# Halves of x, thirds of a transform, and an earlier v: one re-ordering of an attention and long-convolution kernel

## The chip, the cores and the metric

The kernel runs on one core of one Trainium2 chip. (Each run is marked fast or slow; slow means here that it took over 1.5% longer than the fastest run of the same kernel.) Times are device microseconds (us) of that core for one execution of the program.

Engine names: PE is TensorE (matmuls; PEld is its weight load), DVE is VectorE, ACT is ScalarE, POOL is GpSimd, SP is SyncE, whose queue (SPq) issues most DMAs. PSUM is the accumulator memory that PE writes; an "eviction" copies a PSUM tile out to SBUF.

## The reference, cut to what matters

Two independent layers share the launch. Part A is local attention (32 heads of 18 columns, 8 keys per query at distances 0, 2, ..., 14). Part B is a gated long convolution. The outputs are concatenated.

```python
# part A: x (2048 x 576), wqkv (576 x 1728)
q, k, v = split(x @ wqkv)
logits = einsum(q, k gathered at pos - 2*w) * scale        # w = 0..7
o = einsum(softmax(logits), v gathered at pos - 2*w) @ wo
# part B: q, k, v (2048 x 576), ssm_k (576 x 2048)
k_shift = sum over 4 taps of k shifted by t, times shift_k[:, t]
kv = k_shift * v
y = irfft(rfft(kv, 2*S) * rfft(ssm_k, 2*S))[:S] + kv * ssm_D  # computed in float32
return concat([o, q * y])
```

The kernel computes the Fourier transforms as matmuls with tables, in two stages with a trip through Dram between them. The names used below are these. The *first transform* is stage one, over the convolution kernel (k chunks, written to `Dk`) and over `kv` (x chunks, written to `Dx`), eight chunks each. A *k-transform step* (`kh_step`) is stage two of the convolution kernel. A *g step* is stage two of `kv`, the product with the kernel's transform, and the first stage back (tile `Y`, written to `Dy`). There are eight of each. A *P step* (`pv_step`) handles two position groups of the attention's weighted sum: VectorE forms two `P` products and PE sums and projects them.

## The kernel before

The front transposes all of x on PE, then runs 18 q/k matmul steps with the first transform's chunks mixed in. Cuts are marked `# ...`.

```python
for qtr in range(4):                     # all of x is transposed first
    for kp in range(3):
        # ... PE transposes into psA, ScalarE (kp == 1) or VectorE copies to xT

def s1_chunk(src, c2, Dd, vst_pool, add_d):          # one chunk of the first transform
    vst = vst_pool.tile([128, 2, 2 * D], BF16, name="vst")   # pool of 2 buffers
    for ch in range(3):
        ps = psb()                                   # 2 PSUM buffers
        # ... two matmuls
        nc.scalar.activation(vst[:, :, 384 * ch:384 * ch + 384], ps[:, :, 0:384], ACT.Copy)
    for dh, (d0, d1) in enumerate(DCH):
        nc.sync.dma_start(by_f1(Dd, dh, 4 * c2, 4), vst[...][:, :, d0:d1])

wraw = k2[1][...]     # landing place of v's weights: inside a tile of k
sraw = q2[1][...]     # landing place of the shift taps: inside a tile of q

def permute_wv():                                    # v's weights, columns re-ordered
    for kb in range(5):
        nc.scalar.activation(wv[...], wraw[...], ACT.Copy)

sk_step()             # load the taps to sraw, VectorE copies them to skb
load_wv()
permute_wv()
# ...
b_steps = [x chunk 0, k chunk 0, x chunk 1, k chunk 1, ...]
run(qk_steps, b_steps)                               # interleaves the two lists
```

The back half runs the logits with k-transform steps and twelve v steps mixed in, then the softmax, then the P and g steps:

```python
run([logit steps, 8], [ia_tables] + [all 8 kh_steps and v_steps 0..11])
softmax_a(0); softmax_a(1)
g_step(0)
for t2 in range(12, 16): v_step(t2)
halo()                                   # about 2 MB of v copied to neighbours' partitions
softmax_b(0); softmax_b(1)
run([at_step 0..3], [g_step(1)])         # at: the softmax result, transposed
# ...
run([pv_step 0..2], [g_step 2..5])
run([pv_step 3..4], [g_step 6..7])
run([pv_step 5..7], [y_step 0..7])
```

## Time and profile before

The time was 295.15 us (median of 3 runs, 294.57 to 296.24). I cut the span at three events which any version of the kernel has: the first logit product on VectorE, the start of the softmax (the addition of the mask), and the first `P` product.

| phase | ends at (us) | length (us) |
|---|---|---|
| front: loads, q/k, first transform | 107.8 | 107.8 |
| logits | 156.6 | 48.8 |
| softmax, up to the first P product | 190.3 | 33.7 |
| tail | 294.6 | 104.3 |

The page of before opens with the span and each engine's busy time; its second part shows the same busy time in tenths for 40 slices of 7.4 us, with PEclk, the granted TensorE clock, below.

```profile
span 294.6 us, 5101 instructions
...
PE 241.2 (82%) x2129; PEld 152.6 (52%) x2129; DVE 201.3 (68%) x188; ACT 167.5 (57%) x242; POOL 25.9 (9%) x60
...
PE   1579269999997779999999455379999999997993
...
PEclk9999859999999778999999857558999999998999
```

PE is the busiest engine, so the reader should look for where it is *not* busy: at the start, at slices 4 and 5 (counted from 0), around slices 12 to 14, and in the softmax (slices 22 to 25).

The windows view of before gives busy time by phase (start:end, length, then busy time and instruction count of PE, PEld, DVE, ACT and POOL, the granted clock, the DMA share and GB/s).

```profile
0.00:107.80 107.80, 83.49 (x457) 43.62 (x457) 61.65 (x75) 63.95 (x76) 8.75 (x32) 0.92 0.65 207
107.80:156.60 48.80, 47.26 (x486) 27.22 (x488) 43.22 (x31) 32.43 (x55) 0.00 (x0) 0.97 0.51 156
156.60:190.30 33.70, 19.09 (x152) 12.70 (x149) 25.19 (x33) 23.59 (x36) 13.44 (x23) 0.71 0.68 196
190.30:294.60 104.30, 91.37 (x1038) 69.06 (x1037) 71.26 (x53) 47.50 (x76) 3.74 (x5) 0.93 0.48 151
```

The logits phase keeps PE and VectorE both close to full (47.3 and 43.2 of 48.8 us).

The list of waits of before names the stall at slices 4 and 5 (engine, tile and line, whom it waited for, total us, times, longest).

```profile
PE psA L248 <- ACT q L251: 8.1, 1, 8.1
```

The timeline of before shows the cause (start, us, engine, line, operation, tile and source; in brackets the idle time before and what ended it).

```profile
32.29 5.95 ACT L309 ACTIVATE wv<-k 128x576 bf16<-128x576 bf16 x5 [4.15 <-DMA k<-in_A_wqkv_dram]
...
39.34 1.01 PE L248 MATMUL psA<-xT,wq 128*128 128x512 bf16 x2 [8.07 <-ACT q L251]
```

ScalarE first waited 4.15 us for v's weights, then permuted them for 5.95 us. Each engine has its "own instruction stream" (the Trainium skill, "Trainium Architecture — The Big Picture", "Inside one NeuronCore"), and here the trace shows what follows from the order within one: the q/k evictions behind the permutes came late, both PSUM buffers were full, and PE stood until 39.34 us with four q/k steps done.

The chain of waits of before (start, us, what) has one long transfer in the softmax, a `Dy` write that stood behind the halo copies.

```profile
169.52 11.23 DMA Dy<-Y
```

### The profile page before, as it was taken

Reading aid. Unit: us, or ns where it says so; the run is one execution under the profiler, and the core shown is the slowest. Engines: PE = TensorE matmul, PEld = TensorE weight load, DVE = VectorE, ACT = ScalarE, POOL = GpSimd, SP = SyncE. Lnnn points to the kernel's source line nnn. Section 1 sums busy time; section 2 is a strip of 40 time slices with the busy share of each in tenths; the row PEclk is TensorE's granted clock in tenths of the full one; section 3 lists DMA queues with packets and bytes.
Section 4 is the critical chain, followed back from the end, with each engine's and each line's share of the span. In section 5 each row is a group of like instructions: output and inputs, shape, how many; then the busy total and the mean of one; then the engine's idle time right before and its main releaser. Section 6 shows DMA issues by size and latency. Waiting matters only on the chain.

```text
span 294.6 us, 5101 instructions
## 1 busy us (share of the span) xinstructions
PE 241.2 (82%) x2129; PEld 152.6 (52%) x2129; DVE 201.3 (68%) x188; ACT 167.5 (57%) x242; POOL 25.9 (9%) x60
## 2 busy tenths in 40 slices
PE   1579269999997779999999455379999999997993
PEld 1464024555543336565547233168676766766782
DVE  3750895898771149899977991685879669694531
ACT  2422656668868662877877957323576585550311
POOL 8200000000000000000000845000000000012200
PEclk9999859999999778999999857558999999998999
DMA  7999623595555556653344198820442432559982
GB/s 232 360 323 305 234 77 144 178 285 163 160 162 160 160 160 184 222 148 94 103 148 145 40 278 221 283 82 0 123 146 110 149 127 94 184 154 309 328 255 80
DMA packets 42594, 52.37 MB, mean 178 GB/s; under 512 B 2174, under 2 KB 36686, under 8 KB 42445
## 3 DMA queue, kind: packets, MB, share of 16 engines
q1 hardware_dynamic: 39644, 47.04, 50.4%
q0 software_dynamic: 1264, 3.17, 4.3%
q10 hardware_dynamic: 1664, 1.84, 1.9%
q8 instruction: 16, 0.26, 0.3%
q14 instruction: 6, 0.05, 0.0%
HBM read 31.11 MB, written 18.87 MB: 170 GB/s over the span
## 4 chain that ended last, share of the span: by engine, by line
PE 50%; ACT 17%; DMA 16%; DVE 11%; issue 5%; SPq 1%; DVEq 0%; ACTq 0%
PE psA L248 9%; PE psA L235 7%; PE psB L279 6%; PE psA L556 5%; PE psB L454 5%; PE psA L569 5%; DMA out_dram<-m 4%; DMA xnat<-in_A_x_dram 4%; ACT Xc L457 4%; DMA Dy<-Y 4%; DMA k<-in_A_wqkv_dram 4%; PE psB L293 3%; PE psA L398 3%; ACT Y L503 3%; ACT vst L283 3%
## 5 line engine op out<-in xcount | busy, mean ns | idle before, releaser
L248 PE MATMUL psA<-xT,wq 128*128 128x512 bf16 x160 | 42.7, 407 | 8.7 <-ACT q L251 8.1
L556 PE MATMUL psA<-ident,P 128*128 128x128 bf16 (+1 forms) x640 | 46.2, 231 | 1.5 <-DVE P L547 1.4
L556 PEld LDWEIGHTS <-P 128*128 128x128 bf16 (+1 forms) x640 | 40.9, 107 | 8.4 <-issue 4.6
L547 DVE TENSOR_TENSOR P<-vX,at 128x4608 bf16<-128x4608 bf16 x16 | 40.1, 2550 | 4.3 <-PE psA L556 4.3
L283 ACT ACTIVATE vst<-psB 128x768 bf16<-128x768 f32 x48 | 36.3, 814 | 9.1 <-PE psB L279 8.0
L395 DVE TENSOR_TENSOR prod<-q,k 128x4096 bf16<-128x4096 bf16 x16 | 36.1, 2284 | 0.8 <-PE psA L398 0.6
L248 PEld LDWEIGHTS <-wq 128*128 128x128 bf16 x160 | 16.2, 103 | 27.8 <-issue 14.1
L454 PE MATMUL psB<-Wt,W 128*64 128x288 bf16 x256 | 28.0, 312 | 1.5 <-ACT Y L503 0.6
L560 ACT ACTIVATE xT<-psA 128x1024 bf16<-128x1024 f32 x8 | 8.2, 1024 | 34.8 <-PE psA L556 34.8
L500 PE MATMUL psB<-m,IAt 64*128 64x288 bf16 x128 | 14.9, 320 | 14.2 <-DVE m L493 7.6
L235 PE MATMUL psA<-wv,xT 128*128 128x288 bf16 x160 | 25.3, 294 | 0.3 <-ACT vX L237 0.3
L491 DVE TENSOR_TENSOR m<-Xc,Khat 128x2304 bf16<-128x2304 bf16 x8 | 10.8, 1356 | 18.6 <-ACT Xc L457 18.6
L503 ACT ACTIVATE Y<-psB 128x576 bf16<-128x576 f32 x32 | 18.9, 650 | 7.4 <-PE psB L500 6.1
L296 DVE COPY kTt<-psB 128x1152 bf16<-128x1152 bf16 x8 | 6.1, 758 | 24.0 <-PE psB L293 23.9
L569 PE MATMUL psA<-wv,xT 128*128 128x288 bf16 x160 | 22.3, 287 | 0.0
L235 PEld LDWEIGHTS <-xT 128*128 128x128 bf16 x160 | 18.8, 147 | 6.8 <-issue 6.8
L539 POOL DMA_DIRECT2D wv<-in_A_wo_dram x18 | 8.9, 501 | 151.7 <-PE psA L235 146.2
L457 ACT ACTIVATE Khat<-psB 128x576 bf16<-128x576 f32 x32 | 19.5, 653 | 3.4 <-PE psB L454 3.1
L587 DVE TENSOR_TENSOR m<-psB,Lsb 128x576 bf16<-128x576 f32 x16 | 11.4, 752 | 14.6 <-DMA out_dram<-m 8.2
L457 ACT ACTIVATE Xc<-psB 128x576 bf16<-128x576 f32 x32 | 19.6, 651 | 1.3 <-PE psB L454 1.1
L454 PEld LDWEIGHTS <-W 128*64 128x64 bf16 x256 | 12.7, 112 | 13.5 <-issue 11.9
L146 PE MATMUL psA<-ident,xnat 128*128 128x128 bf16 x80 | 9.5, 310 | 11.1 <-DMA xnat<-in_A_x_dram 10.0
(116 smaller groups left out, 331.2 us busy)
## 6 DMA issues: line engine op xcount, KB each, us to landing
Dx<-vst SPq DMA_DIRECT2D x16, 288.0 KB, 3.0
Dk<-vst SPq DMA_DIRECT2D x16, 288.0 KB, 3.0
Wt<-Dk SPq DMA_DIRECT2D x8, 576.0 KB, 3.8
Wt<-Dx SPq DMA_DIRECT2D x8, 576.0 KB, 3.9
Dy<-Y SPq DMA_DIRECT2D x8, 576.0 KB, 3.0
Wt<-Dy SPq DMA_DIRECT2D x8, 576.0 KB, 6.0
kX<-in_B_k_dram SPq DMA_DIRECT2D x3, 1008.0 KB, 5.2
vt<-in_B_v_dram SPq DMA_DIRECT2D x4, 576.0 KB, 8.3
```

Of the source, the lines that this page charges most:

```text
L235: nc.tensor.matmul(ps[:, di, 0:288], xTt[:, kb, t2, :], wv[:, kb, d0:d1], start=(kb == 0), stop=(kb == 4))
L248: nc.tensor.matmul(ps[:, u, :], wcols(kb, comp, ct), xT[:, kb, 512 * j:512 * j + 512], start=(kb == 0), stop=(kb == 4))
L279: nc.tensor.matmul(ps[:, ri, 0:384], T1[:, ri, :], sf[:, 384 * ch:384 * ch + 384], start=True, stop=not extra)
L283: nc.scalar.activation(vst[:, :, 384 * ch:384 * ch + 384], ps[:, :, 0:384], ACT.Copy)
L395: nc.vector.tensor_tensor(prod[:], q2[ct // 2][:], k2[ct // 2][:, :, sh:sh + S], ALU.mult)
L454: nc.tensor.matmul(ps[64 * hp:64 * hp + 64, im, 0:HD], W2[:, im, 8 * g + 2 * prl + hp].rearrange("p l f -> p (l f)"), Wt[:, 2 * prl + hp, ...
L457: nc.scalar.activation(dst[:, :, prl, :], ps[:, :, 0:HD], ACT.Copy, scale=scale)
L500: nc.tensor.matmul(ps[:, hp, 0:HD], IAt[64 * hp:64 * hp + 64, zi, 4 * g + prl, :], m1[64 * hp:64 * hp + 64, zi, prl, :], start=(zi == 0), ...
L503: nc.scalar.activation(Y[:, 2 * prl:2 * prl + 2, :], ps[:, :, 0:HD], ACT.Copy)
L547: nc.vector.tensor_tensor(P[:].rearrange("p w (d h) -> p w d h", h=H), vs, at[:, :, t2, :].unsqueeze(2).to_broadcast([128, W, DH, H]), ALU ...
L556: nc.tensor.matmul(oacc[0:csz, ci, 128 * u:128 * u + 128], Ps[u][:, wi, 128 * ct:128 * ct + csz], ident[:], start=(ci % 2 == 0 and u == 0 ...
L569: nc.tensor.matmul(pso[:, di, 0:288], oT[:, ct, t2, :], wot[:, ct, d0:d1], start=(ct == 0), stop=(ct == 4))
```

## The change

The intent: start q/k on half of x and so fill the 0 to 39 us stretch; weave the first transform in thirds so that its evictions are shared between ScalarE and VectorE, and PE and ScalarE no longer wait for each other in turn at the end of the front; put the wv permutes on GpSimd; let v and its halo copies lead the logits phase so that no halo copy stands in the softmax. Five of the eight k-transform steps are written after the logits to make room; in the compiled order four of them run in the softmax (16 of the 32 `Khat` evictions in the trace of after). The diffs here and below are shortened: helper lambdas and some lines are left out, and `...` marks a cut.

```diff
-    for qtr in range(4):
+    def x_tr(qtr):
 ...
+    x_tr(0)
+    x_tr(1)
 ...
+    def s1_part(src, key, c2, ch, Dd, add_d):       # one third of a chunk
+        if ch == 0:
+            vsts[key] = kvp.tile([128, 2, 2 * D], BF16, name="vst")
 ...
+        if ch == 1:
+            nc.vector.tensor_copy(vst[:, :, 384 * ch:384 * ch + 384], ps[:, :, 0:384])
+        else:
             nc.scalar.activation(vst[:, :, 384 * ch:384 * ch + 384], ps[:, :, 0:384], ACT.Copy)
 ...
-            nc.scalar.activation(wv[...], wraw[...], ACT.Copy)
+            nc.gpsimd.tensor_copy(wv[...], wraw[...])
 ...
     sk_step()
+    qk_steps[0]()
+    qk_steps[1]()
+    x_tr(2)
+    x_tr(3)
     load_wv()
     permute_wv()
 ...
-    run(qk_steps, b_steps)
+    # k and x thirds alternate: k0.0 x2.0 k0.1 x2.1 k0.2 x2.2 k1.0 ...; k transposed 2 chunks ahead
+    run(qk_steps[2:], parts)
 ...
-    run([logit steps], [ia_tables] + mixed)
+    vh = []
+    for c in range(4):
+        vh += v_steps[4 * c:4 * c + 4] + [lambda c=c: halo(c)]
+    run([logit steps], [ia_tables] + vh + [lambda i=i: kh_step(i) for i in range(3)])
 ...
     softmax_a(0)
     softmax_a(1)
+    kh_step(3)
     g_step(0)
-    for t2 in range(12, 16):
-        v_step(t2)
-    halo()
+    kh_step(4)
     softmax_b(0)
     softmax_b(1)
+    for i in range(5, 8):
+        kh_step(i)
     run([at_step 0..3], [lambda: g_step(1)])
```

The q/k tiles also move up in the allocation.

More of the change, by code (lines that the diff above doesn't have):

```diff
@@ L107 @@
     wq = wqp.tile([128, 5, 2 * D], BF16, name="wq")
+    qk = pool("qk", 1, "left")
+    q2 = [qk.tile([128, 2, S], BF16, name=f"q2_{i}") for i in range(2)]
+    k2 = [qk.tile([128, 2, PADL + S], BF16, name=f"k2_{i}") for i in range(2)]
+    qh = qk.tile([128, S // 2], BF16, name="qh")
+    kh = qk.tile([128, PADL + S // 2], BF16, name="kh")
     xin = pool("xin", 4, "left")
@@ L215 @@
     nc.vector.tensor_copy(maskb[:], mask_f[:])
-    tw.release()
-    xin.release()
-    qk = pool("qk", 1, "left")
-    q2 = [qk.tile([128, 2, S], BF16, name=f"q2_{i}") for i in range(2)]
-    k2 = [qk.tile([128, 2, PADL + S], BF16, name=f"k2_{i}") for i in range(2)]
-    qh = qk.tile([128, S // 2], BF16, name="qh")
-    kh = qk.tile([128, PADL + S // 2], BF16, name="kh")
     for i in range(2):
@@ L269, in qk_half_step @@
             nc.scalar.activation(kh[64:128, 0:PADL], ps[64:128, 0, 0:PADL], ACT.Copy)
-    def s1_chunk(src, c2, Dd, vst_pool, add_d):
+    vsts = {}
+    def s1_part(src, key, c2, ch, Dd, add_d):
         sf = src.rearrange("p t d -> p (t d)")
-        vst = vst_pool.tile([128, 2, 2 * D], BF16, name="vst")
-        for ch in range(3):
-            ps = psb()
-            for ri in range(2):
-                extra = add_d and c2 == 0 and ri == 0 and ch < 2
-                nc.tensor.matmul(ps[:, ri, 0:384], T1[:, ri, :], sf[:, 384 * ch:384 * ch + 384], start=True, stop=not extra)
-                if extra:
-                    n = 384 if ch == 0 else 192
-                    nc.tensor.matmul(ps[:, ri, 0:n], row0[:], Db[:, 384 * ch:384 * ch + n], start=False, stop=True)
-            nc.scalar.activation(vst[:, :, 384 * ch:384 * ch + 384], ps[:, :, 0:384], ACT.Copy)
-        for dh, (d0, d1) in enumerate(DCH):
-            nc.sync.dma_start(by_f1(Dd, dh, 4 * c2, 4), vst[:].rearrange("p r (t d) -> p (r t) d", t=2)[:, :, d0:d1])
@@ L287, in k_step @@
-    def k_step(c2):
-        kt = kpre.tile([128, 2, D], BF16, name="kTt", bufs=2)
-        ptr = pb.tile([128, 2, 1024], BF16, name="psB")
-        for u in range(2):
-            for db in range(5):
-                n = 128 if db < 4 else 64
-                nc.tensor.transpose(ptr[:, u, 128 * db:128 * db + n],
-                                    knats[db][0:n, :].rearrange("p (a b) -> p b a", b=NT)[:, 2 * c2 + u, :],
-                                    ident[0:n, 0:n])
-        nc.vector.tensor_copy(kt[:], ptr[:, :, 0:D])
-        s1_chunk(kt, c2, Dk, kvp, True)
+        if ch == 0:
+            vsts[key] = kvp.tile([128, 2, 2 * D], BF16, name="vst")
@@ new lines, in s1_part @@
+        vst = vsts[key]
+        ps = psb()
+        for ri in range(2):
+            extra = add_d and c2 == 0 and ri == 0 and ch < 2
+            nc.tensor.matmul(ps[:, ri, 0:384], T1[:, ri, :], sf[:, 384 * ch:384 * ch + 384], start=True, stop=not extra)
+            if extra:
+                n = 384 if ch == 0 else 192
+                nc.tensor.matmul(ps[:, ri, 0:n], row0[:], Db[:, 384 * ch:384 * ch + n], start=False, stop=True)
+        if ch == 1:
+            nc.vector.tensor_copy(vst[:, :, 384 * ch:384 * ch + 384], ps[:, :, 0:384])
+        else:
+            nc.scalar.activation(vst[:, :, 384 * ch:384 * ch + 384], ps[:, :, 0:384], ACT.Copy)
@@ L299 @@
+        if ch == 2:
+            for dh, (d0, d1) in enumerate(DCH):
+                nc.sync.dma_start(by_f1(Dd, dh, 4 * c2, 4), vst[:].rearrange("p r (t d) -> p (r t) d", t=2)[:, :, d0:d1])
     wraw = k2[1][:].rearrange("p a t -> p (a t)")[:, 0:5 * D].rearrange("p (k c) -> p k c", k=5)
@@ L308, in permute_wv @@
             p0 = 64 if kb == 4 else 0
-            nc.scalar.activation(wv[p0:128, kb, :].rearrange("p (d h) -> p d h", h=H),
-                                 wraw[p0:128, kb, :].rearrange("p (h d) -> p d h", d=DH), ACT.Copy)
+            nc.gpsimd.tensor_copy(wv[p0:128, kb, :].rearrange("p (d h) -> p d h", h=H),
+                                  wraw[p0:128, kb, :].rearrange("p (h d) -> p d h", d=DH))
     v_steps = [lambda t2=t2: v_step(t2) for t2 in range(NT)]
@@ L351, with x_part @@
     kvt = {}
-    def x_step(c2):
-        if c2 % 2 == 0:
+    def x_part(c2, ch):
+        if c2 % 2 == 0 and ch == 0:
             kvt[0] = kv_step(c2 // 2)
-        s1_chunk(kvt[0][:, 2 * (c2 % 2):2 * (c2 % 2) + 2, :], c2, Dx, kvp, False)
+        s1_part(kvt[0][:, 2 * (c2 % 2):2 * (c2 % 2) + 2, :], "x", c2, ch, Dx, False)
     sk_step()
+    qk_steps[0]()
+    qk_steps[1]()
+    x_tr(2)
+    x_tr(3)
     load_wv()
     permute_wv()
+    tw.release()
+    xin.release()
     kpre = pool("kpre", 1, "left")
@@ L368, with k_tr, k_part @@
     nc.gpsimd.dma_start(Db[:], B_ssm_D.partition_broadcast(128))
-    b_steps = [lambda c2=c2: x_step(c2) for c2 in range(8)]
-    for c2 in range(8):
-        b_steps.insert(2 * c2 + 1, lambda c2=c2: k_step(c2))
-    run(qk_steps, b_steps)
+    ktt = {}
+    def k_tr(c2):
+        ktt[c2] = kpre.tile([128, 2, D], BF16, name="kTt", bufs=3)
+        ptr = pb.tile([128, 2, 1024], BF16, name="psB")
+        for u in range(2):
+            for db in range(5):
+                n = 128 if db < 4 else 64
+                nc.tensor.transpose(ptr[:, u, 128 * db:128 * db + n],
+                                    knats[db][0:n, :].rearrange("p (a b) -> p b a", b=NT)[:, 2 * c2 + u, :],
+                                    ident[0:n, 0:n])
+        nc.vector.tensor_copy(ktt[c2][:], ptr[:, :, 0:D])
+    def k_part(c2, ch):
+        if ch == 0 and c2 == 0:
+            k_tr(0)
+            k_tr(1)
+        if ch == 0 and c2 + 2 < 8:
+            k_tr(c2 + 2)
+        s1_part(ktt[c2], "k", c2, ch, Dk, True)
+    parts = []
+    for c2 in range(2):
+        parts += [lambda c2=c2, ch=ch: x_part(c2, ch) for ch in range(3)]
+    for c2 in range(8):
+        for ch in range(3):
+            parts.append(lambda c2=c2, ch=ch: k_part(c2, ch))
+            if c2 < 6:
+                parts.append(lambda c2=c2, ch=ch: x_part(c2 + 2, ch))
+    run(qk_steps[2:], parts)
     kpre.release()
@@ L504, in g_step, with halo @@
         nc.sync.dma_start(by_rt(Dy, dh, g), Y[:])
-    mixed = []
-    for g in range(8):
-        mixed += [lambda g=g: kh_step(g)] + (v_steps[2 * g:2 * g + 2] if g < 4 else v_steps[g + 4:g + 5])
-    def halo():
-        nc.sync.dma_start(vX[1:113, 0:14, :], vX[0:112, 16:30, :])
-        nc.sync.dma_start(vX[113:128, 0:14, :], vX[112:127, 16:30, :])
-        nc.sync.dma_start(vX[0:1, 0:14, :], vX[0:1, 16:30, :])
-    run([lambda wi=wi: logit_step(wi) for wi in range(W)], [ia_tables] + mixed)
+    def halo(c):
+        lo = max(2, 4 * c)
+        src, dst = slice(14 + lo, 18 + 4 * c), slice(lo - 2, 4 * c + 2)
+        nc.sync.dma_start(vX[1:113, dst, :], vX[0:112, src, :])
+        nc.sync.dma_start(vX[112:128, dst, :], vX[111:127, src, :])
+        if c == 3:
+            nc.sync.dma_start(vX[0:1, 0:14, :], vX[0:1, 16:30, :])
+    vh = []
+    for c in range(4):
+        vh += v_steps[4 * c:4 * c + 4] + [lambda c=c: halo(c)]
+    run([lambda wi=wi: logit_step(wi) for wi in range(W)], [ia_tables] + vh + [lambda i=i: kh_step(i) for i in range(3)])
     lg.release()
```

## The prediction

> What bounds the kernel now. TensorE (PE) is busy 82% of the 294.6 us span (busy table), so I ask where it is not. The timeline shows four places. (1) 0 to 21 us: loads and transposes of x. (2) 31.3 to 39.3: q/k matmuls wait 8.1 us for a PSUM buffer (list of waits): ScalarE stood behind five wv permutes (5.95 us) whose load landed at 32.3. (3) 94 to 110: q/k work is used up, the first transform runs alone, PE and ScalarE alternate (0.81 us eviction, two PSUM buffers), VectorE is nearly idle. (4) 160 to 190: softmax, and Y evictions held 11.2 us by a Dy write behind 2 MB of halo copies (chain of waits). Elsewhere PE is full (50 to 90), or VectorE (41 us of logit products); after 205 PE repeats a period of 11.3 us, its own work.
>
> What the change does.
> - wv permutes go to GpSimd: stall (2) goes. But the compiled order also moves the copy of the shift taps to VectorE's tenth place, ahead of every x copy. Its load stands behind x and weights (4.4 MB at 320 GB/s: lands at 15 to 16 us), so x copies start near 17 instead of 7.4. I count: first two q/k steps 22 to 26; second half of x, mixed with tap products of 1.36 us, done by 32 to 33. PE then has two steps done where the old kernel had four, which stopped till 39. Net at 40 us: 2 to 3 us, not 8. GpSimd copies read SBUF while VectorE runs two-input products; the Trainium skill (SBUF — State Buffer, Who interferes with whom) says these block each other (no trace here shows it yet). It may delay the first kv tile by 2 to 4 us.
> - Thirds woven, the middle one evicted by VectorE (estimate 0.85 us), k transposed two steps ahead: PE work left at 33 us is 14 steps of 2.13, halves 5.5, 48 thirds of 0.33, eight k transposes of 1.17: 61 us, at the 95% seen in 50 to 83, 64; plus 5 for start and tail. First transform ends near 103, not 110: minus 6.
> - Logits: v leads, four k-transform steps instead of eight; VectorE needs 44 us. 46 to 47 instead of 48.8: minus 2.
> - Softmax: halo and v steps leave, four k-transform steps move in (16 evictions of 0.6). From last logit to first P product 33.8 us becomes 26.5 (ScalarE-bound): minus 7.
> - Given back: two g steps (3.9 us of PE each) done before the first P now fall in the PE-bound tail of 104 us: plus 3 to 6.
>
> Sum: about minus 11. Predicted 284 us, range 276 to 292. Chances: faster by over 2% 0.76, within 2% 0.21, slower 0.03.
>
> What would show each step: no 8 us q/k wait on ScalarE, but a VectorE wait of about 8 us for the taps, ending at 15 to 16; first q/k matmul at 21 to 23; x transposes finished at 31 to 34; first logit product at 99 to 104; softmax start to first P 25 to 28 us; no Dy write above 6 us; first P to the end 107 to 110.
>
> What would make it wrong: taps landing earlier (gain nearer 18); GpSimd copies far longer than 1 us each, delaying kv tiles and a k eviction near 42; staging buffers with 3 us writes stalling the thirds; more cold clock (0.5 to 0.8 after idle stretches); the tail absorbing the g steps, or y writes lengthening it.

## More of the kernel before

Last, VectorE's timeline of before around the first P product. The letter pattern of the tail is easiest to see here: the g products (`m`, four instructions for one g step) and the `P` products share VectorE in one fixed order.

```profile
186.34 1.36 DVE L491 TENSOR_TENSOR m<-Xc,Khat 128x2304 bf16<-128x2304 bf16 x1 [8.12 <-ACT Xc L457]
...
190.35 7.49 DVE L547 TENSOR_TENSOR P<-vX,at 128x4608 bf16<-128x4608 bf16 x3
202.12 5.03 DVE L547 TENSOR_TENSOR P<-vX,at 128x4608 bf16<-128x4608 bf16 x2 [4.29 <-PE psA L556]
208.51 1.36 DVE L491 TENSOR_TENSOR m<-Xc,Khat 128x2304 bf16<-128x2304 bf16 x1 [1.36 <-ACT Xc L457]
```

The whole order, with g written where the last of a g step's four products stands and P for one P product, is `ggg PPPPP g PP g PP g PP g PP g PPP`. Three g steps are multiplied before the first P.

## The result, and the profile after

The changed kernel took 311.03 us (median of 4 runs, 309.28 to 312.02); the kernel before, run beside it on the same chip, took 294.86 (292.07 to 296.24). The ratio is 1.0555, 95% interval 1.0464 to 1.0646: **slower by 5.5%**. A ratio here and below is the mean time of one kernel's fast runs over that of the other's fast runs of the same rounds, so it is not quite the ratio of the medians quoted.

| phase | before | after | forecast change | measured change |
|---|---|---|---|---|
| front | 107.8 | 117.1 | −6 | +9.3 |
| logits | 48.8 | 46.2 | −2 | −2.6 |
| softmax to first P | 33.7 | 27.2 | −7 | −6.5 |
| tail | 104.3 | 118.9 | +3 to +6 | +14.6 |

Two of four terms came out as forecast, one of them in part by luck (see front_only and back_only). The front has the wrong sign, and the tail is more than twice its upper bound.

The page of after:

```profile
span 309.4 us, 5117 instructions
...
PE 242.5 (78%) x2129; PEld 150.9 (49%) x2129; DVE 217.9 (70%) x204; ACT 153.6 (50%) x221; POOL 34.3 (11%) x65
...
PE   1039699999976659999981685598999999998664
...
PEclk9999799999999655999996578579999999999979
```

PE did the same work (242 against 241 us) in a longer span. The clock row now reads 6, 5 and 5 in slices 13 to 15, where before was at 7 or 8. The windows of after, by the same four phases:

```profile
0.00:117.10 117.10, 84.37 (x473) 44.30 (x474) 79.01 (x91) 50.27 (x59) 17.15 (x37) 0.93 0.61 192
117.10:163.30 46.20, 43.81 (x448) 28.30 (x448) 42.98 (x30) 24.22 (x41) 7.07 (x12) 0.93 0.50 147
163.30:190.50 27.20, 15.55 (x128) 8.40 (x128) 17.20 (x25) 23.21 (x36) 6.38 (x12) 0.69 0.60 183
190.50:309.40 118.90, 98.74 (x1080) 69.90 (x1079) 78.72 (x60) 55.88 (x89) 3.75 (x5) 0.92 0.48 152
```

In the tail PE has 7.4 us more work (98.7 against 91.4), about the two g steps that the prediction named. But the phase is 14.6 us longer.

The list of waits of after has three entries that matter in the front. The old 8.1 us wait of the q/k matmuls is gone from it.

```profile
PE psA L152 <- DVE xT L157: 14.0, 5, 10.5
...
DVE skb L322 <- DMA q<-in_B_shift_k_dram: 11.3, 1, 11.3
...
ACT vst L291 <- DMA Dk<-vst: 8.6, 4, 2.3
```

The first two are one event: VectorE waited 11.3 us for the taps, in front of the copies of x, and PE waited 10.5 us for those copies. (In before VectorE waited 9.4 us for the taps too, but behind all copies of x.) The prediction had this one. The third, an eviction into a staging buffer that waits for that buffer's last write to reach Dram, it had only as a risk. The chain of waits of after runs through it:

```profile
81.57 5.37 DMA Dk<-vst
87.04 0.82 ACT vst L291
...
101.05 3.00 DMA Dk<-vst
104.16 0.82 ACT vst L291
...
109.64 3.02 DMA Dk<-vst
```

VectorE's timeline of after at the first P product:

```profile
190.53 2.56 DVE L580 TENSOR_TENSOR P<-vX,at 128x4608 bf16<-128x4608 bf16 x1 [9.96 <-ACT at L475]
193.01 1.35 DVE L521 TENSOR_TENSOR m<-Xc,Khat 128x2304 bf16<-128x2304 bf16 x1
...
195.55 2.55 DVE L580 TENSOR_TENSOR P<-vX,at 128x4608 bf16<-128x4608 bf16 x1
198.02 0.75 DVE L523 TENSOR_TENSOR m<-m,m 128x1152 bf16<-128x1152 bf16 x1
...
206.79 1.36 DVE L521 TENSOR_TENSOR m<-Xc,Khat 128x2304 bf16<-128x2304 bf16 x1 [4.88 <-ACT Xc L487]
...
218.77 1.36 DVE L521 TENSOR_TENSOR m<-Xc,Khat 128x2304 bf16<-128x2304 bf16 x1 [3.08 <-ACT Xc L487]
```

The order is now `g PP g PP g PP g PP g PP g PP g PP g PP`: one g step is multiplied before the first P, and seven stand behind it, each split by a P product as the lines show. From the first P product to the start of the last `Y` eviction takes 84.8 us (before: 69.7); from there to the end both kernels need 34 to 35 us.

### The profile page after: what moved, and what is told of

It reads as the page before. It is cut to its first block, busy times and chain, and to the rows that moved or that the text cites. A ratio compares the mean times of both kernels' runs of the same rounds, so it can differ in the third digit from the quotient of the medians.

```text
span 309.4 us, 5117 instructions
## 1 busy us (share of the span) xinstructions
PE 242.5 (78%) x2129; PEld 150.9 (49%) x2129; DVE 217.9 (70%) x204; ACT 153.6 (50%) x221; POOL 34.3 (11%) x65
## 3 DMA queue, kind: packets, MB, share of 16 engines
q1 hardware_dynamic: 40126, 47.06, 48.3%
## 4 chain that ended last, share of the span: by engine, by line
PE 47%; DVE 23%; DMA 13%; ACT 11%; issue 2%; SPq 1%; POOL 1%; DVEq 0%; ACTq 0%; POOLq 0%
PE psA L250 9%; PE psA L237 8%; DVE P L580 6%; PE psB L484 6%; PE psA L589 5%; PE psB L284 5%; DMA Dk<-vst 4%; DVE m L521 3%; DVE m L522 3%; PE psB L530 3%; PE psA L428 3%; DMA k<-in_A_wqkv_dram 3%; ACT Y L533 3%; DMA out_dram<-m 3%; ACT Khat L487 2%; ACT vst L291 2%
## 5 line engine op out<-in xcount | busy, mean ns | idle before, releaser
L589 PE MATMUL psA<-ident,P 128*128 128x128 bf16 (+1 forms) x640 | 50.7, 228 | 4.6 <-DVE P L580 4.6
L589 PEld LDWEIGHTS <-P 128*128 128x128 bf16 (+1 forms) x640 | 39.8, 105 | 18.7 <-issue 11.2
L291 ACT ACTIVATE vst<-psB 128x768 bf16<-128x768 f32 x32 | 25.7, 810 | 23.2 <-PE psB L284 12.0
L484 PE MATMUL psB<-Wt,W 128*64 128x288 bf16 x256 | 30.9, 326 | 6.3 <-ACT Xc L487 3.1
L289 DVE CAST vst<-psB 128x768 bf16<-128x768 f32 x16 | 15.3, 957 | 17.6 <-PE psB L284 13.3
L237 PE MATMUL psA<-wv,xT 128*128 128x288 bf16 x160 | 24.8, 302 | 0.5 <-ACT kh L265 0.5
L521 DVE TENSOR_TENSOR m<-Xc,Khat 128x2304 bf16<-128x2304 bf16 x8 | 10.9, 1357 | 20.3 <-ACT Xc L487 20.3
L152 PE MATMUL psA<-ident,xnat 128*128 128x128 bf16 x80 | 8.3, 275 | 21.0 <-DVE xT L157 14.0
L620 DVE TENSOR_TENSOR m<-psB,Lsb 128x576 bf16<-128x576 f32 x16 | 11.5, 753 | 16.1 <-DMA out_dram<-m 10.2
L237 PEld LDWEIGHTS <-xT 128*128 128x128 bf16 x160 | 19.5, 147 | 6.5 <-issue 4.9
L602 PE MATMUL psA<-wv,xT 128*128 128x288 bf16 x160 | 21.6, 286 | 1.2 <-ACT xT L593 0.6
L487 ACT ACTIVATE Xc<-psB 128x576 bf16<-128x576 f32 x32 | 20.6, 656 | 2.4 <-PE psB L484 1.4
L284 PEld LDWEIGHTS <-T 128*128 128x128 bf16 x96 | 9.6, 105 | 23.4 <-issue 18.6
```

What stands on the lines that cost most here:

```text
L237: nc.tensor.matmul(ps[:, di, 0:288], xTt[:, kb, t2, :], wv[:, kb, d0:d1], start=(kb == 0), stop=(kb == 4))
L284: nc.tensor.matmul(ps[:, ri, 0:384], T1[:, ri, :], sf[:, 384 * ch:384 * ch + 384], start=True, stop=not extra)
L484: nc.tensor.matmul(ps[64 * hp:64 * hp + 64, im, 0:HD], W2[:, im, 8 * g + 2 * prl + hp].rearrange("p l f -> p (l f)"), Wt[:, 2 * prl + hp, ...
L487: nc.scalar.activation(dst[:, :, prl, :], ps[:, :, 0:HD], ACT.Copy, scale=scale)
L589: nc.tensor.matmul(oacc[0:csz, ci, 128 * u:128 * u + 128], Ps[u][:, wi, 128 * ct:128 * ct + csz], ident[:], start=(ci % 2 == 0 and u == 0 ...
L602: nc.tensor.matmul(pso[:, di, 0:288], oT[:, ct, t2, :], wot[:, ct, d0:d1], start=(ct == 0), stop=(ct == 4))
```

## The experiments

Fronts and backs are independent pieces of the text, so most experiments combine one front with one back. A short list of what each kernel is made of:

| kernel | front | back | median us, fast runs | ratio to before |
|---|---|---|---|---|
| after | new | new | 311.03 | 1.0555 |
| front_only | new | before's | 302.63 | 1.0271 |
| back_only | before's | new | 302.11 | 1.0216 |
| stage4 | new, 4 staging buffers | new | 299.00 | 1.0149 |
| g1_early | new | new, g step 1 earlier | 311.18 | 1.0530 |
| taps_stage4 | 4 buffers, taps land elsewhere | new | 302.18 | 1.0279 |
| front_fixed | as taps_stage4 | before's | 294.19 | 0.9998 |
| mix_back | before's | third version | 288.25 | 0.9802 |
| fixed_mix | as taps_stage4 | third version | 288.61 | 0.9821 |
| f1_stage4 | 4 buffers, taps and wv land elsewhere | new | 295.15 | 1.0042 |
| f1_2buf | 2 buffers, taps and wv land elsewhere | new | 304.85 | 1.0385 |
| f1_mix | as f1_stage4 | third version | **282.81** | **0.9620** |
| f2_mix | f1_mix, wv permutes back on ScalarE | third version | 283.05 | 0.9649 |

With their 95% intervals and a line at 2%, f1_mix and f2_mix are faster than before, front_fixed and f1_stage4 the same, and after, g1_early, taps_stage4 and f1_2buf slower. front_only, back_only and stage4 are slower, and mix_back and fixed_mix faster, but their intervals cross the 2% line.

### The theories

Theory: two separate losses, adding up. In the front, the thirds of k and x each hold one of the two staging buffers, so a chunk's first eviction must wait for the Dram write of the chunk just before it. In the tail, a g step that is not multiplied before the first P costs a whole period of the P and g loop (about 12 us), not its 3.9 us of PE work. Rival for the front: the late taps alone. Rival for the tail: the P and g loop is bound by its own PE work, and the extra time is the cold clock or the two steps' PE time. Rival for both: one part of the change disturbs the other.

### front_only and back_only: which half loses?

```diff
 front_only: the changed kernel, with everything from the logits on as in before
 back_only:  the kernel before, with everything from the logits on as changed
```

> Only the first half of the change (q/k on half of x, permutes on GpSimd, woven thirds); from the logits on it is the kernel before. Theory T1 (two independent losses: the first transform ends 9.4 us later, the back part costs a net 5.4 = logits -2.5, softmax -6.8, tail +14.7): 304 to 305 us, first logit product still near 117 us, first P product to end back at 104. Rival R1 (the front loss is absorbed later, the whole loss is the tail): about 295 us. Rival R2 (the tail is long only because the front is late, or contention from it): also the whole 311 minus nothing but order, but then back_only is fast.

> The kernel before, with only the order from the logits on changed (v and halo lead, k-transform steps 3 to 7 in the softmax). T1: 300 us, first logit product at 108 as before, first P near 181, first P to end 118 instead of 104. If the tail is long only as a knock-on of the front part (R2): 286 to 288 us, since logits and softmax gain 9 us and nothing is given back.

front_only took 302.63 us in the median of its three fast runs (301.87 to 305.43; the fourth, 308.94, was slow), ratio 1.0271 (1.0182 to 1.0361). Its phases were 115.9, 48.7, 33.4 and 102.1 us. back_only took 302.11 us (300.80 to 302.34), ratio 1.0216 (1.0143 to 1.0289), with phases of 107.3, 48.3, 26.7 and 118.0 us. In each, front, softmax and tail have the changed kernel's length where they belong to the changed half, and before's where they do not, within about 2 us. The logits are the exception: the new order behind the old front takes 48.3 us, hardly less than before's 48.8. The 2.6 us gained there appear only when both halves are new, and no run shows why. By the ratios the two losses are 8.0 and 6.4 us, 14.4 in sum; the whole change lost 16.4, each to within 2 to 3 us. So there are two separate losses, one in each half; an interaction of a few us is not excluded.

### stage4: four staging buffers

```diff
-            vsts[key] = kvp.tile([128, 2, 2 * D], BF16, name="vst")
+            vsts[key] = stg.tile([128, 2, 2 * D], BF16, name="vst")
 ...
+    stg = pool("stg", 4, "left")
```

> The changed kernel with four staging buffers for the thirds instead of two (nothing else). T1a (the end of the first transform is held by the 3 us Dk and Dx writes: x and k each have only one staging buffer): waits of evictions for Dk/Dx writes (15 us in the list now) fall below 3, first logit product at 110 to 112 instead of 117.2, time 304 to 306 us. Rival (PSUM ping-pong and slow VectorE evictions of 0.96 us set the pace): first logit product 115 or later, time 309 to 311.

It took 299.00 us (298.30 to 302.53), ratio 1.0149 (1.0067 to 1.0232): 12 us less than the changed kernel from two more buffers (in a pool of their own), a larger gain than the theory expected (304 to 306). The first logit product came at 107.1 us, 10.0 us earlier. The list of waits no longer has a wait for a `Dk` or `Dx` write. The windows view shows where the 10 us were; the stretch from 80 us to the first logit product, first of after:

```profile
80.00:117.10 37.10, 26.46 (x145) 12.33 (x144) 16.77 (x18) 17.87 (x24) 0.00 (x0) 0.81 0.45 135
```

and of stage4:

```profile
80.00:107.10 27.10, 24.24 (x149) 12.14 (x149) 17.36 (x18) 18.26 (x23) 0.00 (x0) 1.00 0.58 169
```

ScalarE and VectorE do nearly the same work in both. With two buffers PE was idle 10.6 us of this stretch and ran at a clock of 0.81; with four it was idle 2.9 us at a clock of 1.00. The stalls cost twice: the wait itself, and slower matmuls after it. That a TensorE which has idled runs slower until it has been busy for a while is stated by the Trainium skill ("TensorE: Matmul & The Clock Gate", Part 1); this pair of windows agrees, with the k third's matmuls at a mean of 388 ns in after and 326 ns in stage4.

The prediction knew the 3 us of these writes from the profile. They could also have been worked out. The skill ("SBUF — State Buffer", "The DMA setup-cost knee") puts a transfer at about 2 us plus its bytes over 436 GB/s. For the 288 KB of one of these writes that is an estimate of 2.7 us; the profile of before measures 3.0 us. A chunk's writes thus hold its buffer for 3 us, and thirds come faster than that once the q/k steps are used up: in stage4 the last 12 are evicted in 9 us, from 98.9 us on.

### g1_early: one g step out of the tail

```diff
-    kh_step(4)
+    g_step(1)
     softmax_b(0)
     softmax_b(1)
-    for i in range(5, 8):
+    for i in range(4, 8):
         kh_step(i)
-    run([at_step 0..3], [g_step(1)])       # and the loop below from g step 3, not 2
+    run([at_step 0..3], [g_step(2)])
```

> The changed kernel with g step 1 moved ahead of the second softmax half and g step 2 where g step 1 stood, so that one more g step is done before the first P product. T1b (the tail is a loop whose period of 12 us is set by the g chain, and each g step left over costs a whole period): first P later by 3 to 6 us (evictions of g1 on ScalarE), first P to end 107 to 108 instead of 118.9, time 303 to 307 us. Rival (only the longer period counts, 12.0 against 11.3 us, because P products stand between the g products on VectorE; or the y steps' writes): first P to end 115 or more, time 310 to 315.

It took 311.18 us (309.31 to 312.11), the same as after and outside the theory's 303 to 307. Two phases moved, against each other: the tail as far as the theory says, the softmax much further (3 to 6 us were expected). The windows of g1_early for softmax and tail:

```profile
162.60:200.70 38.10, 20.44 (x160) 10.15 (x160) 20.97 (x29) 27.96 (x44) 6.31 (x12) 0.69 0.51 163
200.70:307.60 106.90, 89.86 (x1048) 66.86 (x1047) 75.12 (x56) 49.51 (x80) 3.73 (x5) 0.94 0.50 158
```

The tail fell from 118.9 to 106.9 us (−12.0) for one g step moved out, three times the 3.9 us of PE that the prediction priced it at. But the 12.0 us are not the price of one step alone, for the period of the loop changed with it, from 12.0 us in after (206.79 to 218.77 above) to 11.3 us. VectorE's timeline of g1_early:

```profile
222.04 1.36 DVE L521 TENSOR_TENSOR m<-Xc,Khat 128x2304 bf16<-128x2304 bf16 x1 [1.72 <-ACT Xc L487]
...
233.34 1.36 DVE L521 TENSOR_TENSOR m<-Xc,Khat 128x2304 bf16<-128x2304 bf16 x1 [2.28 <-ACT Xc L487]
```

All five kernels profiled in the fast state with seven g steps left over have the 12.0 us period and a P product inside each g step; the eight with five or six left have 11.3, and at most the first of those g steps is split. Over five periods that is about 3 of the 12.0 us. Nor is it mostly waiting: PE's busy time in the tail fell by 8.9 us (98.7 to 89.9).

The softmax grew from 27.2 to 38.1 us (+10.9). It has no room in this version: it carries four k-transform steps and g steps besides, and in the trace 13 `Khat` evictions in a row, 7.7 us on ScalarE, stand directly in front of the at evictions that the first P waits for. That suggests that the k-transform steps are in the wrong place; mix_back below tests it.

### taps_stage4, front_fixed: a fix that missed

In the changed kernel the taps land in a tile of q (`sraw = q2[1]`), and VectorE reaches the copy of them early. I reasoned that landing them in x's first tile, free once that quarter is transposed, would let the compiled order put them after the x copies.

```diff
-    sraw = q2[1][:].rearrange("p a t -> p (a t)")[:, 0:4 * D].rearrange("p (d j) -> p d j", j=4)
+    sraw = xns[0][:].rearrange("p a c -> p (a c)").rearrange("p (d j) -> p d j", j=4)
```

> stage4 with the shift taps loaded into the memory of the first x tile, so that their load waits for that tile's transposes and the compiled order puts the copy on VectorE behind the x copies of the first half (it stood ahead of all of them). T2 (VectorE standing at that copy until 16.6 us delays everything after it): first q/k matmul at 14 to 16 us instead of 23.8, all x transposed by 29 instead of 36, first logit product at 99 to 102 against 107.1 in stage4, time 290 to 293 against 299. Rival (the first transform is bound by loads of k and v, or by VectorE's own work, so the front's start is hidden): first logit product 105 or later, time 297 or more.

> The same mended front, with the back part of the kernel before. If the phases add as they did so far (front 100, logits 48.8, softmax to first P 33.7, tail 104): 286 to 289 us, faster than the kernel before by 2 to 3%. Rival (a faster front runs into the back's transfers): 292 or more.

taps_stage4 took 302.18 us (301.62 to 302.82), 3 us *more* than stage4; the first logit product was at 108.8 us. front_fixed took 294.19 us (291.71 to 295.67), ratio 0.9998: this front is no better than before's. I had named half of the block. The VectorE timeline of taps_stage4:

```profile
18.46 0.18 DVE L224 CAST maskb<-mask_f 128x32 bf16<-128x32 f32 x1 [9.98 <-POOL mask_f L221]
...
19.67 4.98 DVE L217 CAST Eh<-e_f 128x192 bf16<-128x192 f32 x1 [0.96 <-POOL e_f L91]
```

and GpSimd's own timeline of the same kernel:

```profile
15.17 1.19 POOL L306 COPY wv<-k 64x576 bf16<-64x576 bf16 x1 [10.21 <-DMA k<-in_A_wqkv_dram]
...
21.07 4.61 POOL L306 COPY wv<-k 128x576 bf16<-128x576 bf16 x4
```

GpSimd's compiled order had the first wv permute ahead of the rest of the mask and table work, and that permute waited 10.2 us for the weights. VectorE then waited 9.98 us for the mask table, just as it had waited for the taps. The two blocks stood side by side; with one taken away, the other held the x copies. The second line of VectorE's timeline shows something else: a small copy which took 0.25 us in before took 4.98 us beside GpSimd's work (more in the last section).

### mix_back, fixed_mix: k-transform steps back in the logits

The windows of before show ScalarE a third free in the logits. The third version of the back keeps the early halo but leaves all eight k-transform steps in the logits, two v steps to each.

```diff
-    for c in range(4):
-        vh += v_steps[4 * c:4 * c + 4] + [lambda c=c: halo(c)]
-    run([logit steps], [ia_tables] + vh + [lambda i=i: kh_step(i) for i in range(3)])
+    for g in range(8):
+        vh += [kh_step(g)] + v_steps[2 * g:2 * g + 2] + ([halo(g // 2)] if g % 2 else [])
+    run([logit steps], [ia_tables] + vh)
     softmax_a(0)
     softmax_a(1)
-    kh_step(3)
     g_step(0)
-    kh_step(4)
     softmax_b(0)
     softmax_b(1)
-    for i in range(5, 8):
-        kh_step(i)
```

> The kernel before with only: all 16 v steps and all 8 k-transform steps interleaved 2 to 1 in the logits, halo copies in four pieces as v comes ready, and nothing but g steps 0 and 1 between the softmax halves. T3 (the back part of the change loses because k-transform steps were taken out of the logits, where ScalarE has slack, into the softmax, where they hold ScalarE and push g steps into the tail; early halo copies are good by themselves): logits 49 to 51, softmax to first P 26 to 29, first P to end 105 to 108, time 289 to 293, against 302 for back_only. Rival (early v and halo themselves make the tail long, since the first P product comes before the g steps): first P to end 116 or more, 299 to 303.

> The mended front of taps_stage4 with the back of mix_back. If both halves add: first logit product 100, logits 50, softmax 27, tail 107: 283 to 287 us, 3 to 4% faster than the kernel before. If one of the two does not hold, 290 or more.

mix_back took 288.25 us (287.24 to 289.06), ratio 0.9802 (0.9731 to 0.9874), slightly better than expected. fixed_mix took 288.61 us (288.17 to 289.38), ratio 0.9821: the taps_stage4 front adds nothing here either, which is a miss of that expectation. The windows of mix_back for logits, softmax and tail:

```profile
106.30:158.20 51.90, 51.16 (x518) 31.18 (x519) 43.46 (x30) 35.44 (x59) 1.78 (x3) 0.95 0.58 177
158.20:182.30 24.10, 11.07 (x80) 6.52 (x80) 21.11 (x30) 16.19 (x24) 11.63 (x21) 0.59 0.49 141
182.30:286.20 103.90, 90.19 (x1064) 66.21 (x1063) 75.07 (x56) 51.84 (x84) 3.74 (x5) 0.98 0.52 168
```

The logits are 3.1 us longer than in before (PE is now full, 51.2 of 51.9), the softmax is 9.6 us shorter, and the tail is the same. `Dy` writes take 2.8 us in the median, and the big halo copies come in pieces of 504 KB and 4.4 us. VectorE's order is `gg PPP g PP g PP g PP g PP g PP g PPP`. Six g steps stand behind the first P, one more than in before, and the stretch from the first P to the last `Y` is 70.0 us against 69.7. So the price of a left-over g step is not a constant: the sixth cost 0.3 us (in before, five P products ran with no g step among them, so there was a place), and the seventh (after against g1_early) 12, the longer period included.

### f1_stage4, f1_2buf, f1_mix: both blocks taken away

v's weights are now also loaded into tiles of x, so that their permutes stand last on GpSimd, behind the tables.

```diff
-    wraw = k2[1][:]...
+    wraw, wraw4 = xns[1], xns[2][:, 0, :]        # besides the taps in xns[0]
```

> taps_stage4 failed because GpSimd stood at the first wv permute (load landed at 15.2) ahead of the tables that VectorE needs, and one VectorE copy then took 5 us beside GpSimd's permutes. Here wv is also loaded into x tiles (1 and 2), so that the permutes stand last on GpSimd, behind all tables. T2' (two in-order blocks at once, taps on VectorE and wv on GpSimd, held the front): first q/k matmul at 14 to 16 us, x all transposed by 27 to 30, first logit product at 100 to 103 against 107.1, time 291 to 295 against 299 for stage4. Rival (the first transform is bound elsewhere: VectorE's tap products, loads of the second k operand): first logit product 106 or later, time 298 or more.

> The same unblocked front in the changed kernel as it was, with two staging buffers. If blocks and staging buffers cost independently: first logit product 110 to 112 (117.1 less the 6 or so that f1_stage4 gains over stage4), time 303 to 306. If the staging waits take up all that the front gains: first logit product 115 or more, 309 or more.

> The unblocked front with four staging buffers and the back of mix_back. If the phases add (first logit product 102, logits 50, softmax to first P 24, tail 104): 279 to 283 us, 4 to 5% faster than the kernel before. If the front's gain does not hold: 287 or more, as fixed_mix.

f1_stage4 took 295.15 us (294.80 to 296.37), ratio 1.0042. The first q/k step began at 14.1 us (after: 23.75), q/k resumed at 31.1 us, and the first logit product came at 102.4 us, 5.4 us before the old kernel's and 4.7 us before stage4's. This is the front that the prediction had hoped for (99 to 104 us).

f1_2buf, the same with two staging buffers, took 304.85 us in the median of its three fast runs (303.91 to 307.70), ratio 1.0385. The fourth execution took 715.72 us, which nothing here explains; the profile fell on that one, so I do not read it, and the expected first logit product could not be checked. By the fast runs, taking the blocks away is worth about 5 us with two buffers (after's ratio 1.0555 to 1.0385) and about 3 us with four (1.0149 to 1.0042); each ratio is good to 2 to 3 us, and within that the two losses of the front look independent.

f1_mix, this front with the third back, took 282.81 us (282.42 to 283.85), ratio 0.9620 (0.9561 to 0.9678). **It beats both kernels**: by 11 us the kernel before that ran beside it (293.96), and by 28 us the changed kernel's 311.03 of an earlier set of runs. Its phases are 102.5, 49.6, 24.1 and 104.5 us.

### f2_mix: does the sharing between GpSimd and VectorE cost anything?

```diff
-            nc.gpsimd.tensor_copy(wv[...], ...)
+            nc.scalar.activation(wv[...], ..., ACT.Copy)
```

> This is f1_mix with one edit: the permutes of wv run on ScalarE again instead of GpSimd. Theory (sharing with GpSimd costs on the path): in f1_stage4 the five permutes ran at 26.2 to 36.5 us on GpSimd and VectorE's two-input steps of 1.36 us took 1.45 to 2.37 us in that stretch; without them the k and v tile is ready 2 to 3 us earlier, the first logit product stands at 99 to 101 us instead of 102.5, and the time is 279 to 282 us. Rival (the permutes cost more in ScalarE's order than they cost beside VectorE, as in the kernel before where each took about 1.2 us of ScalarE and waited for wv's load): the first logit product is at 103 us or later and the time is 283 us or more.

It took 283.05 us (282.68 to 283.23), ratio 0.9649 (0.9602 to 0.9696), with the first logit product at 103.2 us. The rival's prediction held: no gain. The mechanism of the theory is there all the same, and off the critical path. VectorE's timeline of f1_mix (GpSimd copies from 26.2 to 36.6 us), with one tap product and the last product of the first `kv` tile:

```profile
33.17 2.36 DVE L339 TENSOR_TENSOR tA<-kX,skb 128x2304 bf16<-128x2304 bf16 x1
...
39.26 1.36 DVE L345 TENSOR_TENSOR tA<-tA,vt 128x2304 bf16<-128x2304 bf16 x1
```

and of f2_mix (no GpSimd work in that stretch), the same two and the wait that follows:

```profile
32.84 1.35 DVE L339 TENSOR_TENSOR tA<-kX,skb 128x2304 bf16<-128x2304 bf16 x1
...
36.88 1.36 DVE L345 TENSOR_TENSOR tA<-tA,vt 128x2304 bf16<-128x2304 bf16 x1
...
41.76 0.96 DVE L289 CAST vst<-psB 128x768 bf16<-128x768 f32 x1 [2.24 <-PE psB L284]
```

The `kv` tile is 2.4 us earlier without the copies, and then VectorE waits 2.24 us for PE: its next `vst` copy starts at 41.76 us, and at 41.80 in f1_mix. The gain became slack. In this front the runs show no difference between the two engines as place of the permutes; taps_stage4 against f1_stage4 shows that the place in the engine's order does.

## Why the prediction was wrong

**The stalls of the front: right in kind, somewhat late in time.** The 8 us q/k wait went; the taps held VectorE until 16.6 us (forecast 15 to 16); the first q/k matmul came at 23.75 us (21 to 23) and PE had two q/k steps done where the old kernel had four. x was transposed at 36.6 us rather than 31 to 34. The cause was put down to the taps alone; taps_stage4 showed that GpSimd's order was a second block of nearly the same length (10.0 us beside 11.3).

**"First transform ends near 103, not 110: minus 6": wrong; measured 117.1 us.** This is the first failed step. It was made of 33 us for the start and 64 plus 5 us for the work left. The start was 3.6 us late (36.6), and the work took 80.5 us. The prediction priced the PE work, at PE's usual occupancy, and kept the two staging buffers out of the sum; it named "staging buffers with 3 us writes stalling the thirds" as a risk and gave it no number. stage4 gave it one: with four buffers the same work took 70.5 us from 36.6 on, close to the 69 forecast, and the time fell by 12 us. The weave caused it. In the old kernel the chunks alternate whole, so a buffer comes round after a whole other chunk's time. With k and x thirds alternating, both buffers are open at once and each is wanted again one third after it is sent off. (Of the 9.3 us by which the front grew, 6.7 are this stage: PE's last first-transform matmul ended at 116.8 us against 110.1. The rest is the cut: in before ScalarE evicts the whole stage, and VectorE begins the logits 2.4 us before PE has finished it.)

**Logits, "46 to 47": the number right** (46.2), the reason not shown: the same logits order behind the old front took 48.3 us (back_only), and the old order behind the new front 48.7 (front_only). **Softmax, "26.5" and "no Dy write above 6 us": right** (27.2; the longest `Dy` write is 4.9 us).

**"Two g steps (3.9 us of PE each) ... plus 3 to 6": wrong; measured 14.6 us.** The count was right: three g steps were multiplied before the first P in before and one in after, and PE's work in the tail grew by 7.4 us. This is the second failed step: the price, taken as PE work alone. After the first few products the P and g loop has one g step to a pair of P products in VectorE's order. A g step which finds no free place among the early P products lengthens the loop; g1_early measured 12.0 us for one, about 3 of it because the period is 12.0 us with seven steps left and 11.3 with six. The other 2.6 us of the 14.6 lie between g1_early (106.9) and before (104.3), which has one step fewer left. Of the whole 14.6, 7.4 are PE's busy time and 7.2 its idle time. Why the period lengthens, no run isolates.

**The choice behind both terms: moving k-transform steps into the softmax.** The prediction took the 7 us saved in the softmax for granted as a gain. Those steps had filled ScalarE's slack in the logits at little cost. In the softmax they keep ScalarE busy (23.2 of 27.2 us) exactly where the old kernel worked off its second and third g step. mix_back put them back: the logits grew by 3.1 us against before, the softmax shrank to 24.1, the tail stayed, and the sum is 2% faster than before.

**GpSimd "may delay the first kv tile by 2 to 4 us": right in size and of no consequence.** f2_mix measured 2.4 us against f1_mix, whose front is not quite the predicted one, and it fell on slack there.

What stays open: the f1_2buf profile is unusable; how much of mix_back's gain comes from the early halo and how much from the v steps' new place was not separated; neither the 12.0 us period nor the logits' 2.6 us has an isolated cause.

## What to carry to other kernels

When a producer is cut finer and two of them are interleaved, count the buffers behind them again: here two open streams ran freely with one buffer each to fill and one to drain, and the wait for the drain is a Dram write, here 3 us, that shows in no engine's work. Work moved out of a phase is only a gain if it did not sit in another engine's slack there, and a step left over for a periodic loop can cost much more than its work on the busiest engine, here up to 12 us against 3.9, if the loop has no free place for it. When a wait at the head of an in-order engine is removed, look at what stands second: another engine's first instruction may be waiting just as long.

## What the Trainium skill lacked or had wrong

- "SBUF — State Buffer", "Who interferes with whom": the stated rule, that a VectorE instruction with two SBUF inputs contends with a GpSimd instruction that reads SBUF, agrees with the runs: a product took 2.36 us beside the GpSimd copies of f1_mix and 1.35 us in f2_mix without them, and the GpSimd copies took 2.34 us instead of 1.19. What the page lacks is how long the loser can lose. Its summary says that the second to issue blocks until the first finishes; in taps_stage4 a 128x192 float32 to bf16 cast on VectorE (one SBUF input, so it would have to be the page's rule on 2-port modes instead), 0.25 us in before, took 4.98 us, while GpSimd ran a memset and then copies of about 1.2 us in a row (4.61 us for four, not lengthened). The cast ended only with the third copy: VectorE seems to have lost several turns running. front_fixed, with the same front, has the same 4.98 us; in after and stage4 the cast took 1.56 us beside the memset alone. No run isolates it.
- "GPSIMD Engine Reference", 4.1 Engine selection, calls one-input work on GpSimd "roughly line-rate". This case agrees where the GpSimd copies are not lengthened: 1.19 us for a 128x576 bf16 copy with permuted columns (taps_stage4), against 1.24 us on ScalarE (f2_mix). That section does not say that the same copy can take twice as long, 2.34 us, beside two-input VectorE work (f1_mix).
- "TensorE: Matmul & The Clock Gate", Part 1, has nothing that these runs contradict. It puts the ramp penalty at under 1% of a typical kernel's span, but that is the warm-up at the start; it goes on to clocks that fall again in mid-kernel when matmuls wait. That is what is seen here: a granted clock of 0.81 over 37 us of after's front where stage4 had 1.00, and 0.59 to 0.71 over the softmax of the four kernels whose phases are shown. The cost in time was not isolated from the waits, so no share of the span can be given for it.
- No page that I used says what two streams through one small buffer pool cost when the drain is a Dram write. The 2 us fixed cost on the SBUF page makes it foreseeable (estimate 2.7 us, measured 3.0 us for 288 KB); here it was worth 12 us of 311.
